# Delta-rule attention and an MLP on one core: odd heads loaded with batch halves swapped, the first chunk's inverse in half units

## The chip, the cores and the metric

The kernel runs on one core of one Trainium2 chip. The metric is device time in microseconds for one execution; the time before is the median of three runs.

## The reference, cut to what matters

Two stages follow each other. The first is a delta rule over 768 steps, for 4 batches and 8 heads of width 48; the second is an MLP over the 3072 tokens that result.

```python
k_n = k / (np.linalg.norm(k, axis=-1, keepdims=True) + 1e-06)
state = np.zeros((B, H, D, D))                         # B, H, S, D = 4, 8, 768, 48
for t in range(S):
    y[:, :, t] = np.einsum('bhd,bhde->bhe', q[:, :, t], state)
    v_old = np.einsum('bhde,bhd->bhe', state, k_n[:, :, t])
    state = state + beta[:, :, t, None, None] * np.einsum('bhd,bhe->bhde', k_n[:, :, t], v[:, :, t] - v_old)
x = y.transpose(0, 2, 1, 3).reshape(B * S, H * D)      # 3072 x 384
out = gelu_tanh(x @ w_in) @ w_out                      # d_ff = 2048
```

## The kernel before

The 768 steps are cut into 12 chunks of 64. A chunk holds 4 batches x 8 heads x 64 steps; two batches are stacked on the 128 partitions (index `a`, 64 rows each), and the other batch index `x` makes two **units** per chunk, so there are 24 units `u` of 8 heads. Heads are numbered by `g` (pair, 0 to 3) and `p` (even or odd within the pair). Work is bf16, sums are float32 in PSUM.

For each unit, `prep(u)` does this. `kn`, `kb`, `qb` make normalised k, k times -beta, and q in token layout (tile `tok`); `T` and `kT` (units 0 to 5, on TensorE with a copy) or `turn` (later units, a transposing DMA on SP) bring them to `kT`. `G2` and `G` (L542, L534) are the products of keys with keys and of keys with queries; `ln` and `wp` are their masked copies. Then comes the inverse of the chunk's triangular matrix, by five Newton steps: `A` multiplies, `rt` (L603, DVE) subtracts from two times the identity, `B` multiplies again, `bde`, `xi` and `bdc` copy the result back to be the next left factor. In units 2 and up these are full-array matmuls on block-diagonal tiles `bd` (L596); `X1` makes the first one. In units 0 and 1 (`TILED`) they run as 64x64 matmuls on two corners of the array (`At`, `Bt`, L567; start `X1t`, L558).

For each chunk, `chain(c)` does this. `K` (L642) multiplies keys by the state, `R` subtracts v, `Um` or `U` (L665) applies the inverse, `S` (L675) makes the state's update, `Q` (L642) multiplies queries by the state and `O` (L689) adds the part inside the chunk. `On` copies to `xo`, then `turnx` (a transposing DMA, L702) or `X` (six transposes on TensorE, L710, for chunks 0, 1 and 11) make `xT`.

In a 64x64 matmul the row half is set by the partitions of the operands and the column half by the partitions of the output. `K`, `Q` and `S` use all four combinations. `O` reads rows `hf(a)` and writes rows `hf(a)`, so it uses the two diagonal corners.

For each chunk the MLP runs as 16 `up` steps (L731, three matmuls of 256 columns each), four `gelu` on ACT, and two times four `down` steps (L743, four matmuls of 384 columns), with `Z` copies and `out` DMAs. The weights W1 and W2 come in two halves each, on GpSimd's DMA queue: `w1.-2.9` is the half that `up.N.5` and `up.N.75` need, `w1.-3` the half for `up.N` and `up.N.25`. In a label such as `up.5.25/0` the first number is 2c+3 for chunk c; for `K`, `Um`, `S` it is 2c+0.5, for `Q` and `O` 2c+0.6 and 2c+0.7, for `X` and `turnx` 2c+0.8.

q, k and v are loaded by SP (the first chunk's k also by ACT): one DMA for each of `a` = 0, 1, with all 16 heads of both units, in pieces of 192 bytes. Each has a ring of three chunks. `norms` takes squares, sums, root (`pow`: on ACT for the first three chunks, on GpSimd later) and reciprocal. The first root needs another activation table than the copy `tmpl` ahead of it.

The order on each engine is written out by hand, as the lists `ORDER["pe"]`, `["act"]`, `["dve"]`, `["pool"]`, `["sp"]`; `BANKS` gives the PSUM banks in order. Each engine works its list strictly in order and waits at each entry for what it reads. `fill` entries (71 of them, L428) are matmuls on zeros that only fill idle time on TensorE before W1 is there.

The lines around O, before:

```python
def at(name, P, r, b, x, g):
    o = 512 * b + 4 * D * x + D * g
    return P(ps(name))[r, o:o + D]
...
def omat(e, P):
    for x, g in each:
        for p in range(2):
            for a in range(2):
                ins = e.matmul(at("O", P, hf(a), p, x, g), wp[ss[x]][hf(a), 4 * p + g, C:2 * C], ub[hf(a), x, p, g, :],
                               start=first and x == 0 and g == 0, stop=True, skip_group_check=True)
```

Of the kernel before, what the change touches and what calls it, by code (L numbers as in the profile page):

```python
# [30 lines left out]
        A32.4/0 up.5.5/0 up.5/3 up.5.5/1 up.5.5/2 A16.5/0 up.5.5/3 B.4/4 A.6/0 B.5/3 down.6.5/0 B.6/0 down.6.54/0 A32.5/0 G2.8/0
        G2.7/0 A.6/1 B.5/4 down.6.58/0 G.8/0 down.6.62/0 Um.4.5/0 B.6/1 Q.4.6/0 G.7/0 O.4.7/0 G2.9/0 A.6/2 A.8/0 down.6/0 A.7/0 B.6/2
        G.9/0 B.8/0 down.6.04/0 B.7/0 down.6.08/0 A.9/0 A16.6/0 A.8/1 down.6.12/0 A.7/1 B.9/0 B.8/1 up.7.25/0 B.7/1 up.7.25/1 B.6/3
        up.7/0 up.7.25/2 up.7/1 up.7.25/3 A32.6/0 up.7/2 A.7/2 up.7/3 A.9/1 A.8/2 S.4.5/0 up.7.5/0 B.9/1 up.7.5/1 B.7/2 up.7.75/0
        up.7.5/2 up.7.75/1 up.7.5/3 up.7.75/2 A16.7/0 up.7.75/3 A.9/2 K.6.5/0 B.7/3 B.6/4 B.8/2 B.9/2 down.8/0 A32.7/0 down.8.04/0
        B.7/4 down.8.08/0 A16.8/0 down.8.12/0 Um.6.5/0 B.8/3 Q.6.6/0 G2.10/0 O.6.7/0 G.10/0 A16.9/0 down.8.5/0 G2.11/0 S.6.5/0 G.11/0
        down.8.54/0 down.8.58/0 B.9/3 A32.8/0 A.10/0 down.8.62/0 K.8.5/0 B.10/0 B.8/4 up.9.75/0 up.9.25/0 up.9.75/1 up.9.25/1
        up.9.75/2 A.10/1 up.9.75/3 A32.9/0 up.9.25/2 A.11/0 B.10/1 up.9.25/3 up.9.5/0 B.9/4 up.9.5/1 G2.13/0 up.9.5/2 up.9.5/3 G.13/0
        Um.8.5/0 Q.8.6/0 B.11/0 A.10/2 G.12/0 G2.12/0 O.8.7/0 A.13/0 B.10/2 up.9/0 up.9/1 B.13/0 A.11/1 up.9/2 A16.10/0 up.9/3 A.12/0
        B.11/1 A.13/1 S.8.5/0 B.10/3 B.13/1 B.12/0 A.11/2 down.10/0 A.12/1 down.10.04/0 B.11/2 down.10.08/0 up.11.75/0 B.12/1  # L40
        up.11.75/1 A.13/2 up.11.75/2 up.11/0 up.11.75/3 B.13/2 up.11/1 A.12/2 A32.10/0 up.11/2 up.11.25/0 up.11/3 up.11.25/1 A16.11/0
        up.11.25/2 B.12/2 up.11.25/3 up.11.5/0 B.11/3 down.10.12/0 up.11.5/1 K.10.5/0 B.10/4 up.11.5/2 A32.11/0 A16.13/0 up.11.5/3
        down.10.5/0 B.11/4 A16.12/0 down.10.54/0 B.13/3 B.12/3 down.10.58/0 Um.10.5/0 down.10.62/0 G2.14/0 Q.10.6/0 S.10.5/0 O.10.7/0
        G.14/0 A32.13/0 down.12/0 A32.12/0 down.12.5/0 B.13/4 down.12.04/0 A.14/0 down.12.08/0 G2.15/0 G.15/0 K.12.5/0 down.12.54/0
        B.12/4 down.12.12/0 B.14/0 down.12.58/0 Um.12.5/0 down.12.62/0 up.13.75/0 Q.12.6/0 G2.17/0 O.12.7/0 G.17/0 up.13.75/1 A.15/0
        up.13.75/2 up.13/0 A.14/1 up.13/1 up.13.75/3 up.13/2 up.13.5/0 up.13/3 up.13.5/1 B.15/0 up.13.5/2 B.14/1 up.13.5/3 up.13.25/0
        G.16/0 G2.16/0 up.13.25/1 up.15.5/0 up.13.25/2 S.12.5/0 up.13.25/3 up.15.5/1 A.15/1 up.15.5/2 A.16/0 A.14/2 up.15.5/3 A.17/0
        B.15/1 down.14/0 B.16/0 B.14/2 down.14.04/0 B.17/0 A.16/1 down.14.08/0 A.15/2 down.14.12/0 A.17/1 B.16/1 up.15/0 B.15/2
        up.15/1 B.17/1 up.15/2 A16.14/0 A16.15/0 up.15/3 up.15.25/0 A.16/2 up.15.25/1 B.14/3 up.15.25/2 A.17/2 up.15.25/3 B.15/3
        B.16/2 K.14.5/0 A32.14/0 up.15.75/0 B.17/2 up.15.75/1 G2.18/0 up.15.75/2 A16.16/0 up.15.75/3 A32.15/0 A16.17/0 B.14/4 B.16/3  # L50
        B.15/4 down.16/0 G.18/0 G2.19/0 down.14.5/0 Um.14.5/0 down.14.54/0 B.17/3 down.16.04/0 S.14.5/0 G.19/0 Q.14.6/0 down.14.58/0
        down.16.08/0 A.19/0 A.18/0 O.14.7/0 K.16.5/0 down.14.62/0 A32.17/0 B.18/0 B.19/0 down.16.12/0 down.16.5/0 B.17/4 A.18/1
        A32.16/0 down.16.54/0 A.19/1 down.16.58/0 B.18/1 G2.20/0 G.20/0 B.16/4 down.16.62/0 up.17.5/0 B.19/1 up.17.5/1 Um.16.5/0
        up.17.5/2 A.20/0 up.17.5/3 up.17.75/0 G2.21/0 up.17.75/1 B.20/0 up.17.75/2 up.17.25/0 up.17.75/3 up.17.25/1 A.19/2 up.17.25/2
        A.20/1 up.17.25/3 Q.16.6/0 G.21/0 O.16.7/0 up.17/0 B.19/2 up.17/1 A.18/2 up.17/2 B.20/1 up.17/3 A16.19/0 B.18/2 S.16.5/0
        A.21/0 B.19/3 down.18/0 A.20/2 down.18.04/0 B.21/0 A16.18/0 B.20/2 down.18.08/0 A.21/1 down.18.12/0 B.18/3 A16.20/0 A32.19/0
        B.21/1 up.19/0 up.19.5/0 up.19/1 B.20/3 up.19/2 B.19/4 up.19/3 up.19.5/1 A.21/2 up.19.5/2 K.18.5/0 up.19.5/3 B.21/2 A32.18/0
        down.18.5/0 up.19.25/0 B.18/4 up.19.25/1 A16.21/0 G2.22/0 up.19.25/2 Um.18.5/0 up.19.25/3 down.18.54/0 B.21/3 Q.18.6/0 G.22/0
        G2.23/0 O.18.7/0 A32.20/0 down.18.58/0 up.19.75/0 down.18.62/0 up.19.75/1 A.22/0 up.19.75/2 down.20/0 up.19.75/3 B.22/0 G.23/0
        S.18.5/0 down.20.04/0 B.20/4 down.20.08/0 A.23/0 A32.21/0 A.22/1 down.20.12/0 B.23/0 up.21.5/0 B.22/1 up.21.5/1 up.21.75/0  # L60
        B.21/4 up.21.5/2 up.21.75/1 A.23/1 up.21.5/3 K.20.5/0 up.21.75/2 B.23/1 up.21.75/3 up.21.25/0 A.22/2 up.21/0 up.21.25/1
        up.21/1 B.22/2 A.23/2 up.21.25/2 up.21/2 up.21.25/3 B.23/2 down.20.5/0 Um.20.5/0 up.21/3 down.20.54/0 A16.22/0 A16.23/0
        down.20.58/0 B.22/3 down.22.5/0 B.23/3 down.22.54/0 Q.20.6/0 S.20.5/0 O.20.7/0 down.20.62/0 A32.23/0 A32.22/0 K.22.5/0
        down.22/0 B.23/4 down.22.04/0 B.22/4 down.22.58/0 down.22.08/0 Um.22.5/0 down.22.12/0 Q.22.6/0 down.22.62/0 O.22.7/0 up.23.5/0
        up.23/0 up.23.5/1 up.23/1 up.23.25/0 up.23.5/2 up.23/2 up.23.5/3 up.23/3 up.23.25/1 X.22.8/0 up.23.25/2 up.23.75/0 up.23.25/3
        up.23.75/1 down.24/0 up.25.75/0 up.25.25/0 up.25.75/1 up.25.25/1 up.25.75/2 up.23.75/2 up.25.75/3 up.25.25/2 up.23.75/3
# [243 lines left out]
def bass_deltanet__then__act_gelu_tanh_kernel(  # L310
# [13 lines left out]
    NU = 2 * NC  # L324
    DIRECT = lambda u: (2, 3, 4, 5) if u < 8 else (2, 4)
    GROUPS = [[c] for c in range(NC)]
    TURN, TURNX, TILED = 6, 2, 2

    F = Flow()
    A = F.add  # L330

    with nc.allow_non_contiguous_dma("strided loads"), nc.allow_low_precision("bf16 pipeline"):
# [39 lines left out]
        def hf(a, n=C):  # L372
            return slice(64 * a, 64 * a + n)
# [437 lines left out]
```

## Time and profile before

| | before |
|---|---|
| median of 3 runs | 265.88 us (265.6 to 266.23) |
| profiled execution | 266.2 us, span 264.4 us |
| PE, DVE, ACT, POOL busy | 253.8, 202.0, 174.8, 144.5 us |
| granted TensorE clock | 1.0 |
| `fill` on PE | 71, 21.8 us |
| DMAs issued by SP | 148 |
| HBM read, written | 20.64 MB, 4.72 MB |

The span runs from the first to the last instruction; the rest of the profiled execution's time lies around it. PE is TensorE; a matmul is counted busy from its start to its modelled end, and neighbours overlap. A line of a group gives the source line, engine, operation, what it writes and reads, its shape, the count, then busy time and the mean of one in ns, then idle time ahead of it and who ended that. In the slices each digit is a fortieth of the span in tenths. "SPq" and "POOLq" are the queues of SP and GpSimd.

### The profile page before, as it was taken

The page shows a single profiled execution, that of the slowest core. Times are in us where ns is not written, and L with a number is a line of the kernel's source. Part 1 is how long each engine was busy: PE and PEld are TensorE (multiplying, and loading weights), DVE is VectorE, ACT ScalarE, POOL GpSimd, SP SyncE. Part 2 cuts the span into 40 slices and gives each one's busy share as a digit, 9 for nine tenths or more (in the row PEclk, how much of TensorE's full clock was granted, in tenths as well). Part 3 has the DMA queues.
Part 4 walks back from the last instruction along what each step waited for, and adds up shares of the span by engine and source line. Part 5 has one row for each costly group of instructions (what it writes and reads, how often), then busy time and mean ns, then how long its engine had stood idle before and what let it go on. Part 6 is the DMA issues. An engine that isn't in the chain of part 4 may idle for free.

```text
span 264.4 us, 12466 instructions
## 1 busy us (share of the span) xinstructions
PE 253.8 (96%) x5629; PEld 191.6 (72%) x5629; DVE 202.0 (76%) x317; ACT 174.8 (66%) x264; POOL 144.5 (55%) x220
## 2 busy tenths in 40 slices
PE   7899998999899999999999999999999999999994
PEld 2557566877677876877886888877888878778762
DVE  8899796978899999899779888889886876551000
ACT  3758676777886894498663468935788657556431
POOL 8633698849899889875855674480635222110000
PEclk9999999999999999999999999999999999999999
DMA  5996999999999999948997589238149064044023
GB/s 105 175 154 124 146 204 193 177 134 151 158 164 155 141 162 137 188 88 165 169 173 100 125 165 147 48 81 144 25 63 180 5 133 82 2 35 101 6 47 72
DMA packets 117908, 31.86 MB, mean 120 GB/s; under 512 B 111968, under 2 KB 117088, under 8 KB 117856
## 3 DMA queue, kind: packets, MB, share of 16 engines
q1 hardware_dynamic: 113968, 27.63, 69.7%
q0 software_dynamic: 2880, 3.15, 7.6%
q8 instruction: 44, 0.72, 1.2%
q10 hardware_dynamic: 1008, 0.30, 0.5%
q14 instruction: 8, 0.07, 0.1%
HBM read 20.64 MB, written 4.72 MB: 96 GB/s over the span
## 4 chain that ended last, share of the span: by engine, by line
PE 78%; DVE 7%; DMA 5%; ACT 2%; SPq 2%; issue 2%; POOL 2%; POOLq 0%; ACTq 0%
PE ps L743 23%; PE ps L731 21%; PE ps L596 18%; DMA W<-in_moe_w_in_dram 4%; PE ps L428 3%; PE ps L567 3%; PE ps L642 2%; DMA kraw<-in_k_dram 2%; DVE ln L546 2%; PE ps L689 2%; SPq L523 2%; PE ps L534 2%; PE ps L665 1%; DVE rt L603 1%; PE ps L542 1%
## 5 line engine op out<-in xcount | busy, mean ns | idle before, releaser
L731 PE MATMUL ps<-xT,W 128*128 128x256 bf16 x576 | 82.4, 273 | 0.8 <-DMA W<-in_moe_w_in_dram 0.7
L376 ACT ACTIVATE bd<-ps 64x512 bf16<-64x512 f32 x111 | 64.5, 589 | 18.0 <-PE ps L596 16.0
L743 PE MATMUL ps<-W,gT 128*128 128x384 bf16 x384 | 76.3, 326 | 0.0
L736 ACT ACTIVATE gT<-ps 128x1024 bf16<-128x1024 f32 x48 | 48.4, 1021 | 27.0 <-PE ps L731 26.6
L731 PEld LDWEIGHTS ps<-xT,W 128*128 128x128 bf16 x576 | 48.7, 98 | 9.5 <-DMA W<-in_moe_w_in_dram 1.0
L603 DVE TENSOR_TENSOR rt<-ps,two 128x512 bf16<-128x512 f32 x66 | 44.2, 687 | 10.6 <-PE ps L596 9.9
L590 POOL COPY bd<-xi 64x256 f32<-64x256 f32 x64 | 25.1, 394 | 42.4 <-ACT xi L376 30.2
L743 PEld LDWEIGHTS ps<-W,gT 128*128 128x128 bf16 x384 | 32.3, 97 | 15.0 <-ACT gT L736 0.2
L586 POOL TENSOR_SCALAR_AFFINE_SELECT bd<-ln 64x512 bf16<-64x512 bf16 x44 | 28.9, 658 | 22.5 <-DVE ln L546 18.4
L376 DVE CAST bd<-ps 64x512 bf16<-64x512 f32 x45 | 30.8, 686 | 5.1 <-PE ps L596 3.9
L552 DVE CAST_PREDICATED wp<-mup,ps 128x1024 bf16<-128x1024 uint16 (+1 forms) x26 | 29.3, 1133 | 2.3 <-PE ps L534 2.3
L489 POOL TENSOR_TENSOR nrm<-nrm,half 128x16 f32<-128x16 f32 x9 | 26.3, 2929 | 2.1 <-DVE nrm L486 1.9
L376 ACT ACTIVATE xi<-ps 128x512 bf16<-128x512 f32 x31 | 18.3, 594 | 12.1 <-PE ps L596 6.9
L596 PE MATMUL ps<-rt,bd 128*128 128x64 bf16 x528 | 25.5, 194 | 0.3 <-DVE rt L603 0.2
L596 PE MATMUL ps<-wp,bd 128*128 128x64 bf16 (+1 forms) x528 | 24.7, 188 | 1.0 <-issue 0.5
L596 PEld LDWEIGHTS ps<-wp,bd 128*128 128x128 bf16 x528 | 21.3, 97 | 5.5 <-issue 1.1
L596 PEld LDWEIGHTS ps<-rt,bd 128*128 128x128 bf16 x528 | 21.1, 98 | 5.0 <-DVE rt L603 2.4
L603 DVE TENSOR_TENSOR rl<-ps,two 128x384 bf16<-128x384 f32 (+1 forms) x44 | 20.8, 485 | 4.8 <-PE ps L596 4.4
L428 PE MATMUL ps<-wz 128*128 128x512 bf16 x71 | 21.8, 413 | 1.3 <-DVE wz L382 1.2
L510 POOL TENSOR_TENSOR tok<-kraw,nrm 128x384 bf16<-128x384 f32 x21 | 17.6, 841 | 8.4 <-DVE nrm L493 8.1
L546 DVE CAST_PREDICATED ln<-mlo,ps 128x512 bf16<-128x512 uint16 x24 | 16.5, 687 | 4.9 <-PE ps L542 4.6
L512 POOL TENSOR_TENSOR tok<-tok,bsb 128x384 bf16<-128x384 bf16 x21 | 17.5, 836 | 2.7 <-DVE tok L510 1.9
(98 smaller groups left out, 334.5 us busy)
## 6 DMA issues: line engine op xcount, KB each, us to landing
qraw<-in_q_dram SPq DMA_DIRECT2D x24, 192.0 KB, 5.1
vraw<-in_v_dram SPq DMA_DIRECT2D x24, 192.0 KB, 4.9
out_dram<-ob SPq DMA_DIRECT2D x47, 96.0 KB, 2.6
kraw<-in_k_dram SPq DMA_DIRECT2D x22, 192.0 KB, 5.3
W<-in_moe_w_in_dram POOLq DMA_DIRECT2D x2, 768.0 KB, 9.2
W<-in_moe_w_out_dram POOLq DMA_DIRECT2D x2, 768.0 KB, 10.8
kraw<-in_k_dram SPq DMA_DIRECT2D x3, 96.0 KB, 4.0
kT<-tok SPq DMA_TRANSPOSE x18, 5.0
```

The source lines that it names most:

```text
L376: return e.activation(out, in_, ACT.Copy) if e is nc.scalar else e.tensor_copy(out, in_)
L428: return e.matmul(P(f"fill{i}")[:, :], wz[:, 0:128], wz[:, 0:512])
L489: e.tensor_tensor(nr[:, 1, hx], nr[:, 0, hx], half[:, hx], ALU.pow),
L546: A("dve", z + "ln", lambda e, P: e.copy_predicated(ln[m][:, :, :].rearrange("p (x g) t -> p x g t", x=2), mlo[:, :].bitcast(U16).unsqueez ...
L552: A("dve", z + ("wp" if nh == 2 else "wph"), lambda e, P, cs=cs, nh=nh: e.copy_predicated(wp[s][:, :, cs], mup[:, cs].bitcast(U16).unsquee ...
L586: A("pool", z + "X1", lambda e, P, src=src, dst=dst: e.affine_select(out=dst, in_=src, compare_op=ALU.not_equal, fill=1.0, base=0, pattern ...
L590: A("pool", z + "bdc", lambda e, P, src=src, dst=dst: e.tensor_copy(dst.bitcast(F32), src.bitcast(F32)), reads=[w("xi")], writes=[n(f"bd{a ...
L596: ins = e.matmul(P(name)[:, C * h + lo:C * h + C], bd[s][:, h, :], rhs[:, h, lo:C])
L603: A("dve", z + f"rt{lo or str()}", lambda e, P, i=i, lo=lo, r_=r_: e.tensor_tensor(r_[:, :, lo:C], P(ps(f"A{i}")).rearrange("p (h t) -> p ...
L731: ins = e.matmul(P(ph)[:, w * f:w * f + w].rearrange("p (x t) -> p x t", x=2), W1[:, j, 128 * (i + f):128 * (i + f) + 128], x_[:, :, j, :] ...
L736: A("act", z + "gelu", lambda e, P, i=i, ph=ph: e.activation(g_[:, i:i + nf, 0:w], P(ph).rearrange("p (f t) -> p f t", f=nf), ACT.Gelu_app ...
L743: ins = e.matmul(P(po)[:, 0:DM], g_[:, f, 128 * b:128 * b + 128], W2[:, f, :], start=(f == 0), stop=(f == FC - 1))
```

## The change

Five things are done together.

1. **Loads.** For odd heads (`p` = 1) the two stacked batches change places: rows `hf(a)` hold batch `a ^ p`. So each load becomes four DMAs, one for each `p` and `a`, of half the size; beta's copy follows the same pattern in four pieces. With the batches swapped, `O` and `Q` write odd heads to rows `hf(a ^ p)`, so that `O` uses all four corners and its output stands in the right order. `K`, `S` and the inverse work as before on swapped rows.
2. **First chunk in halves.** In units 0 and 1 the transposes, the products, the masked copies, all five Newton steps and their copies are cut into two halves of four heads (`Ath`, `Bth`, `rth`, `xih`, `lnh`, `wphh`, `X1h`), each with a PSUM bank of its own; U, O, X and their copies of chunk 0 are cut by unit `x` (`Uh`, `Oh`, `Xh`, `Unh`, `Onh`, `xTh`).
3. **Table.** `tmpl` now reads `one`, which `tabS` writes, so that the root's table is loaded first.
4. **`TURNX`** goes from 2 to 1: chunk 1's output is turned by DMA on SP, not on TensorE.
5. **Orders and banks** are new for all engines. `fill` goes from 71 to 59 entries, SP's DMAs from 148 to 220. Copies are placed anew between ACT and DVE (`bde` on DVE 45 to 39, on ACT 111 to 117).

The core of the diff:

```diff
-    TURN, TURNX, TILED = 6, 2, 2
+    TURN, TURNX, TILED, SPLIT = 6, 1, 2, 2
...
-                    for a in range(2):
+                    for p, a in quad:
+                        dst = raw[n][s][hf(a), :, :].rearrange("t (x g p) d -> t p x g d", x=2, p=2)[:, p, xs]
...
-                          lambda e, P, n=n, a=a, xs=xs, view=view: e.dma_start(raw[n][s][hf(a), xs, :], view[a, c, :, xs, :]), ...
+                          lambda e, P, a=a, p=p, xs=xs, dst=dst, view=view: e.dma_start(dst, view[a ^ p, c, p, :, xs]),
...
-                A("pe", z + "T", trans, reads=[n("tok0"), n("tok1"), n("tok2"), "ident"], alloc=(ps("T"), 2), mode="m", pos=u, mm=12)
+                for ys, tn in (((0, 1), "T"), ((2,), "Tq")) if u < SPLIT else (((0, 1, 2), "T"),):
...
+                    for y, _, k_ in halves:
+                        def product(e, P, name, rhs, lo, y=y):
+                            for h in range(4):
+                                for a in range(2):
+                                    ins = e.matmul(P(name)[hf(a), C * h + lo:C * h + C], xi[m][hf(a), 4 * y + h, :], rhs[hf(a), 4 * y + h, lo:C])
...
-                        ins = e.matmul(at(name, P, hf(a), p, x, g), kT[ss[x]][hf(p, D), y, g, hf(a)], so[hf(p, D), a, x, g, :],
+                        ins = e.matmul(at(name, P, hf(a ^ p if y else a), p, x, g), kT[ss[x]][hf(p, D), y, g, hf(a)], so[hf(p, D), a, x, g, :],
...
-            def omat(e, P):
+            def omat(e, P, xs=(0, 1)):
                 for x, g in each:
-                    for p in range(2):
-                        for a in range(2):
-                            ins = e.matmul(at("O", P, hf(a), p, x, g), wp[ss[x]][hf(a), 4 * p + g, C:2 * C], ub[hf(a), x, p, g, :],
-                                           start=first and x == 0 and g == 0, stop=True, skip_group_check=True)
+                    for p, a in quad if x in xs else ():
+                        ins = e.matmul(at("O", P, hf(a ^ p), p, x, g), wp[ss[x]][hf(a), 4 * p + g, C:2 * C], ub[hf(a), x, p, g, :],
+                                       start=first and g == 0, stop=True, skip_group_check=True)
```

The new orders where the prediction speaks of them:

```diff
 pool
-  ... X1t.0/0 X1t.1/0 kn.3/0 kb.3/0 kb.2/0 kn.4/0 w1.-2.9/0 X1.2/1 X1.2/0 qb.5.01/0 X1.3/1 w1.-3/0 kn.5/0 X1.3/0 pow.6/0 w2.-2/0 ...
+  ... X1h.0/0 X1h.0/1 X1h.1/1 bdz.3/0 X1h.1/0 kn.3/0 kn.2/0 qb.3.01/0 kb.2/0 X1.2/0 X1.2/1 w1.-2.9/0 X1.3/1 qb.4.01/0 X1.3/0 sq.6/0 w1.-3/0 w2.-2/0 ...
 pe
-  ... X.0.8/0 B.2/1 A.3/0 fill/64 fill/65 fill/66 up.3.5/0 A.2/2 B.3/0 up.3.5/1 B.2/2 up.3.5/2 fill/67 up.3.5/3 up.3.25/0 A.3/1 S.0.5/0 ...
+  ... S.0.5/0 Xh.0.8/1 G.4/0 B.2/1 fill/53 fill/54 A.3/1 up.3.5/0 up.3.5/1 A.2/2 B.3/1 up.3.5/2 fill/55 up.3/0 B.2/2 up.3/1 A.3/2 up.3.5/3 ...
```

More of the change, by code (lines that the diff above doesn't have):

```diff
@@ new lines @@
+        xih.0/4 xih.1/3 sq.4/0 kT.2/0 pow.4/0 xih.0/5 ladj16.-0.2/0 kT.3/0 xih.0/7 xih.1/7 xih.1/6 xih.0/6 R0.0.5/0 xih.0/9 xih.0/8
+        Unh.0.5/0 R0.0.5/1 bde.2/0 bde.2/1 Onh.0.7/0 Unh.0.5/1 sq.8/0 xTh.0.8/0 Onh.0.7/1 bde.3/1 tabG.3/0 S0.0.5/0 xTh.0.8/1 bde.2/2
+        bde.2/3 bde.3/3 bde.2/4 gelu.3.5/0 gelu.3/0 gelu.3.25/0 bde.2/6 bde.3/4 bde.3/5 gelu.3.75/0 bde.4/0 bde.3/6 bde.4/1 bde.2/9
+        bde.2/8 bde.3/8 bde.4/3 Un.2.5/0 On.2.7/0 sq.12/0 bde.4/5 bde.4/4 sq.10/0 bde.5/1 bde.5/0 sq.14/0 Z.4.5/0 bde.4/6 bde.5/3
@@ L115 @@
-        Sn.20.5/0 rt32.23/0 rt32.22/0 R.22.5/0 bde.22/4 Z.22/0 xT.22.8/0 Z.24.5/0
+        wz.-200/0 bdz.4/0 pad.-9/0 bdz.2/0 bdz.7/0 one.-40/0 sqh.0/0 identf.-29/0 sumh.0/0 eps.0/0 ladj16.0.8/0 inv.0/0 kn.0/0
+        betaN.-28/2 betaN.-28/3 betaN.-28/1 betaN.-28/0 ladj16.2.8/0 kb.0/0 sumh.1/0 eps.1/0 inv.1/0 kn.1/0 kb.1/0 lnh.0/1 lnh.0/0
+        wphh.0/0 sum.-140/0 wphh.0/1 lnh.1/1 rth.0/0 lnh.1/0 rth.0/1 eps.-140/0 wphh.1/1 wphh.1/0 inv.-140/0 qT.0/0 rth.0/3 rth.1/1
+        rth.0/2 rth.1/0 kb.3/0 ladj16.1.8/0 rth.1/3 rth.0/4 rth.1/2 wph.1/0 rth.0/5 xih.1/2 wph.0/0 ladj32.2.8/0 sum.4/0 rth.1/4
@@ L116 @@
+        bde.21/3 bde.18/4 rt16.21/0 Un.18.5/0 Z.18.5/0 ln.22/0 wp.22/0 ln.23/0 rt32.21/0 rt.22/0 bde.21/4 wp.23/0 Sn.18.5/0 rt.23/0
+        rt32.20/0 rt.22/1 bde.23/0 bde.20/4 rt.23/1 R.20.5/0 rt.22/2 rt.23/2 rt16.22/0 rt16.23/0 Z.20.5/0 xi.22/1 Sn.20.5/0 rt32.22/0
+        rt32.23/0 R.22.5/0 bde.23/5 On.22.7/0 xT.22.8/0
     """,
     "pool": """
[L118 to L119 removed]
@@ L410, in preset @@
                 A("pool", "0tmplz", lambda e, P: e.memset(tmpl[:, C:2 * C], 0.0), writes=["tmplz"], pos=-11)
-                A("act", "0tmpl", lambda e, P: e.activation(tmpl[:, 0:C], two[:, :], ACT.Copy, scale=-0.5), reads=["two"],
+                A("act", "0tmpl", lambda e, P: e.activation(tmpl[:, 0:C], two[:, :], ACT.Copy, scale=-0.5), reads=["two", "one"],
                   writes=["tmpl"], pos=-11)
@@ L618, in chain @@
             n = lambda y: [f"{y}{s}" for s in ss]
[L619 to L620 removed]
+            inv = n("bd0") + n("bd1")
             ps = lambda y: f"{y}.{c}"
@@ L636, in at @@
                 o = 512 * b + 4 * D * x + D * g
-                return P(ps(name))[r, o:o + D]
+                return P(ps(name) if name != "O" or not first else ps(f"O{x}"))[r, o:o + D]
             def ks(e, P, y, name):
```

429 lines of the change are left out of this document (230 added, 199 removed), and 16 rows, old and new, of the table BANKS.

## The prediction, made before any run of the changed kernel

> **What bounds the kernel now.** I read the busy table and the slices first, then the chain of waits, then the groups by form, then the timelines of TensorE (PE) and of the queues.
>
> ```profile
> PE 253.8 (96%) x5629; PEld 191.6 (72%) x5629; DVE 202.0 (76%) x317; ACT 174.8 (66%) x264; POOL 144.5 (55%) x220
> ...
> DMA  5996999999999999948997589238149064044023
> ```
>
> PE is busy for 96% of 264.4 us. Busy is not yet pace, so I looked at spacing in the timeline: three `up` matmuls start 0.33 us before the next instruction and four `down` ones 0.65 us, early and late alike. After the prologue PE works near its own pace. The second line shows DMA full (nines) from 6.6 to about 105 us.
>
> ```profile
> 33.33 9.55 DMA W<-in_moe_w_in_dram
> 42.93 0.50 PE ps L731 x3
> 45.55 0.76 PE ps L731 x6
> ```
>
> This is the chain that ended last. Up to 42.93 us it waits for one half of W1 (`w1.-3`), issued by GpSimd at 33.33; from there it is nearly all PE. So the end is set by when W1 lands and by how much PE work is left then.
>
> ```profile
> L642 PE MATMUL ps<-st,kT 48*64 48x48 bf16 x704 | 9.7, 189 | 0.0
> ...
> L689 PE MATMUL ps<-us,wp 64*64 64x48 bf16 x384 | 8.3, 187 | 0.3
> ...
> L675 PE MATMUL ps<-us,tok 64*64 64x48 bf16 x352 | 4.8, 188 | 0.2 <-ACT us L376 0.2
> ```
>
> Groups by form: K and Q (L642), O (L689), S (L675) are all 32 matmuls of 48 columns. O uses two corners of the array, the others four. One O takes 8.3/12 = 0.69 us, one S 4.8/11 = 0.44, one K or Q 9.7/22 = 0.44.
>
> **O on four corners.** Chunks 1 to 11 have one O each in the PE-bound part: 11 x (0.69 - 0.44) = 2.8 us less. The first chunk's O lies in the prologue and counts there. Against it could count that the new O lets both row halves write each bank, where S keeps them apart; if the halves then wait for each other, O stays at 0.69. A row speaks to that: the first chunk's U (L665, 64*64) has both row halves writing one bank on two corners, and its 32 take 0.7 us; the full-array Um takes 6.2/11 = 0.56 us for 16, of which some 0.16 is the tail that S loses when another tiled step follows (0.28 to the next start, against its 0.44), so 25 ns each. One after the other, 32 would take 0.96: the halves overlap while sharing a bank. The Trainium skill, TensorEngine Tiling (Array Packing), Gotcha 1, says that different row tiles cannot access the same PSUM bank simultaneously; by that O would stay at 0.69, and U's row does not agree with it. I take 0.44 and keep 0.69 as a rival.
>
> **Transposes of chunk 1.** X.2.8 leaves PE (six matmuls, 61.48 to 61.81 in the timeline): 0.33 us less. It becomes `turnx.2.8` on SP, whose others issue in 1.2 and land in 3.1 us. Between O.2.7 and the next `up` the new order has six `down` (3.9 us), six A or B steps of 0.23, and G and S: over 6 us, against 0.8 (copy) + 3.1 plus any queueing. Hidden if SP comes to it in time; if not, PE waits for the difference.
>
> **The head of the kernel.** `tabS` first removes the 1.28 us table load that stands between sum and root at 5.93. But k of chunk 0 now comes in four quarters per half, two behind each other on each queue: issue at 1.6 plus 4.0 to land is 5.6, against 4.2 to start with before (work on it began at 4.77). 5.6 + 0.49 (square) + 0.55 + 0.21 + 0.18 + 0.18 + 0.56 (kn) and steps between gives 8.3 instead of 8.8. The four betaN of half size (two took 0.73) and kb end near 10.0 instead of 10.52. The halved transposes and the copy of 1024 elements on ACT (1.04) bring `lnh.0` to 12.2 to 12.9, say 12.6, against 13.35.
>
> **The first inverse in halves.** DVE is what it runs on. From `ln.0` to the end of `ln.2` it took 27.70 - 13.35 = 14.3 us. After: 23 operations of 256 elements at 0.34 (row of 128x256: 0.42 busy, 0.08 of it overlapped) = 7.8; four of 192 at 0.28 = 1.1; two `wph` 1.2; two sums 1.7; small norms 0.5; qT and kb.3 0.75; three `ladj` 0.45; a `tri` 0.4; `ln.2` 0.6: 14.5 us, so it ends at 27.1, with a few waits 27.1 to 28. Splitting gives each chain shorter steps, but as many elements and more starts on the busy engine. `X1.2` (two of 0.66) then lets `w1.-2.9` go at 28.5 to 29.5 on POOL; it went at 28.72. `w1.-3` comes after X1.3, qb.4 and now sq.6 (1.46): ln.3 ends near 29.7, so 33 to 34 instead of 33.33. The first half landed at 37.5 and the second followed 5.4 later, so an issue up to about 35 costs nothing. W1 thus lands at 42.9 to 43.7: I take 0.4 us later.
>
> Ahead of it much is gained and not cashed: rt.2, wp.3 and two copies (2.4) after 29.7, then U, Unh, Oh, Onh, Xh, xTh in halves (2.7 against 5.3 from U to `up` before) put `up.3.5/0` at 34.8 instead of 39.38, but its half of W1 lands at 37.5, and the new order asks for the other half (`up.3/0`) three `up` later, near 39. PE then waits 4 us. What it did before the wait differs from the old list by S, A.3/1, B.3/1 (+0.83) less B.2/2 and an `up` (-0.56): 0.27 us less left. The twelve fills removed covered idle time and cost nothing.
>
> **Loads cut in two.** 72 more DMAs on SP (148 to 220), as many bytes and packets. With nothing queued an issue takes 0.6 us whether it carries 192 or 96 KB, so SP has up to 43 us more to issue. Adding up its timeline gives 19 of the first 20 us, 18 of the next 40, 85 of the 100 us from 60 to 160, and 37 after. Many early issues are long (1.0 to 2.3 us) because the full DMA queues push back, and that part is set by bytes. I take nothing for it, at most 5 us.
>
> **Other orders.** DVE hands some 5 us of copies after the prologue to ACT and SP (bde 45 to 39 at 0.69, two xT, one Un), which can take a little from waits on DVE near 113 to 120 us. I take nothing for it; a saving of up to 1 us lies in the range.
>
> **Sum.** -2.8 - 0.33 - 0.27 + 0.4 = -3.0 us. The profiled execution took 266.2 (span 264.4 and 1.8 around it), 0.3 above the median 265.88, so 263.2 on its scale and 262.9 on the median's; I say 263.1. A measurement of this kernel can tell about 0.2% (0.53 us) from no change.
>
> **Rivals.**
> - W1 comes sooner. If the halved chains reach `ln.2` 2 to 3 us earlier (each half operation at 0.25 rather than 0.34 saves 2), W1 is issued and lands as much earlier: 260.6. Against it: the DVE rows show no such rate from PSUM, and W1's two halves need 14 us of shared DMA. 10%.
> - The idle gap slows PE's clock. The first 15 fills take 5.23 us, the 11 from 8.00 take 2.55, so 15 at that later pace take 3.5: a cold start costs about 1.8 us. At the end the granted clock in the windows is 1.00 up to 264.0 and 0.98 in the last 0.4, some 3.5 us after PE's last matmul. A wait of 4 us at `up.3/0` could bring one more slow start: 265.0. No wait in this trace is that long, so nothing shows it mid-kernel. The Trainium skill, TensorE: Matmul & The Clock Gate, HAM oscillation, states as a rule that PE gaps should stay below about 3.4 us, and by it this would happen. 14%.
> - O gains nothing: both row halves wait for each other at the shared bank, and 2.8 stays: 265.9, no change. 6%.
> - Slower: SP becomes the bound from 60 to 160 us. About half of the extra loads fall there; at 0.6 us, 36 of them add 21 to the 85, which makes 106 of 100. SP is in order, so `turn` (landing 5.0) and `turnx` come up to 6 us late by the end of that stretch, and PE waits at G2 and `up`: 263.1 + 5 = 268. It decides where halved loads keep 0.6 us and the pushed-back part (some 27 us: the 85 less 51 loads and stores at 0.6, 14 `turn` at 1.4 and 6 `turnx` at 1.2) shrinks by less than 6. For it: the queue's order is fixed, and DVE, ACT and POOL also wait in order for what it loads. Against: the push-back should shrink by more than that. 18%.
>
> **Chances.** The forecast has 52%. Faster by over 0.2%: 0.52 + 0.10 + half of the clock case (0.07) = 0.69. Within: 0.07 of the clock case and 0.04 of O = 0.11. Slower: SP 0.18 and 0.02 of O with a late W1 = 0.20. The range holds the forecast with the early-W1 end, the clock case, O and the start of the SP case: 260.2 to 266.9.
>
> **What would show it.** Right: O (32 matmuls) at 0.44 us in the groups by form; `lnh` of unit 0 near 12.6; `w1.-2.9` issued near 29 and the `up` after it waiting for W1 until 43 with some 4 us idle; PE busy total down by the fills and O; the chain still PE after 43. Wrong: O at 0.69; W1 landing before 41 or after 45; granted clock below 1.00 near 44; PE idle before L542 or L731 with DMA named between 60 and 160 us, or chain shares of SPq and DMA above the present 2% and 5%.

## The result, and the profile after

The changed kernel takes 276.8 us against 266.1 beside it: ratio 1.040 (95% interval 1.033 to 1.047). It is slower by some 11 us; 263.1 was forecast, and the range ended at 266.9. The profiled execution took 277.71 us, its span 276.0. (Runs in which the chip was disturbed are left out of all ratios; medians hold them.)

The busy table, the granted clock, the DMA share and the shares of the chain, from the page of the changed kernel; the second fence has the chain's line of the kernel before:

```profile
PE 254.1 (92%) x5643; PEld 190.5 (69%) x5643; DVE 196.6 (71%) x327; ACT 178.6 (65%) x279; POOL 145.8 (53%) x226
...
PEclk9999986999999979999999999999999999999999
DMA  6877899989998988897776947646608622124004
...
PE 66%; DMA 13%; POOL 8%; SPq 6%; issue 2%; ACT 2%; DVE 1%; POOLq 0%; ACTq 0%
```

```profile
PE 78%; DVE 7%; DMA 5%; ACT 2%; SPq 2%; issue 2%; POOL 2%; POOLq 0%; ACTq 0%
```

PE is busy for as long as before in a span 11.6 us longer. Its share of the chain fell from 78% to 66%; DMA rose from 5 to 13, SP's queue from 2 to 6, POOL from 2 to 8. Many of the nines of the DMA row have become sevens and eights: the transfers fill their engines less, though more of them are issued.

The chain of waits, the pieces in order of time (start, us, what):

```profile
29.45 8.46 DMA kraw<-in_k_dram
37.99 1.41 POOL sq L497
39.40 8.76 DMA W<-in_moe_w_in_dram
...
59.36 1.42 SPq L470
61.49 4.70 DMA kraw<-in_k_dram
66.37 5.04 DMA xT<-xo
...
91.41 5.08 DMA xT<-xo
```

Where before had one wait for W1 there are now loads. k of chunk 3, the last of its four DMAs issued at 29.45, lands 8.5 us later; `sq.6` on POOL needs it and stands in front of `w1.-3`, which goes at 39.40, not 33.33. DVE, in order, stands at `sum.6` until 39.49 (the first line below, with 4.66 us idle ahead of it), with `rt.2/1` behind it (the second), and PE behind that:

```profile
39.49 1.81 DVE L498 TENSOR_REDUCE nrm<-sq 128x16 f32<-128x768 f32 x2 [4.66 <-POOL sq L497]
41.22 0.68 DVE L635 TENSOR_TENSOR rt<-ps,two 128x512 bf16<-128x512 f32 x1
```

Then SP's own issues (SPq) are a piece of the chain, and `turnx.2.8` and `turnx.4.8` (66.37, 91.41) come late. What PE waited for between 34 and 100 us (us in total, times, longest), and the windows around 40 us and behind the second late `turnx` (third number from the end: granted clock):

```profile
PE ps L782 <- DMA xT<-xo: 4.7, 2, 3.2
PE ps L758 <- DVE rt L635: 2.7, 1, 2.7
PE ps L716 <- issue: 2.2, 1, 2.2
```

```profile
38.00:40.00 2.00, 0.30 (x13) 0.20 (x13) 0.51 (x1) 1.36 (x3) 2.00 (x2) 0.89 0.55 102
40.00:42.00 2.00, 0.00 (x0) 0.00 (x0) 2.00 (x4) 0.23 (x1) 1.98 (x3) 0.50 0.76 106
42.00:44.00 2.00, 1.66 (x28) 1.20 (x29) 1.35 (x2) 0.49 (x1) 2.00 (x1) 0.50 1.03 182
44.00:46.00 2.00, 2.00 (x15) 1.23 (x14) 1.03 (x2) 1.18 (x2) 1.83 (x4) 0.50 1.07 185
```

```profile
97.00:100.00 3.00, 3.00 (x34) 2.43 (x32) 0.00 (x0) 1.66 (x3) 1.38 (x3) 0.60 0.90 159
```

The granted clock is half from 40 to 46 us; PE is idle for the first 2 of these and works at half its clock for the rest. Behind the 3.2 us that PE waited for `turnx.4.8` it falls again, to 0.60 between 97 and 100 us. By `down.4.12`, at 62.05 us before, the changed kernel is 6.5 us behind, by `down.8`, at 95.88 before, 11.4; after that it stays there (11.5 at the end).

The groups by form: K and Q, O, S.

```profile
L673 PE MATMUL ps<-st,kT 48*64 48x48 bf16 x704 | 9.7, 188 | 0.0
L729 PE MATMUL ps<-us,wp 64*64 64x48 bf16 x384 | 5.6, 188 | 0.4 <-issue 0.3
L716 PE MATMUL ps<-us,tok 64*64 64x48 bf16 x352 | 5.2, 188 | 2.3 <-issue 2.2
```

O did nearly what was said of it: 5.6/12 = 0.47 us in place of 0.69, where 0.44 was forecast.

### The profile page after: what moved, and what is told of

Its sections match the earlier page's. It is cut to its first block, busy times and chain, and to the rows that moved or that the text cites. A ratio compares the mean times of both kernels' runs of the same rounds, so it can differ in the third digit from the quotient of the medians.

```text
span 276.0 us, 12596 instructions
## 1 busy us (share of the span) xinstructions
PE 254.1 (92%) x5643; PEld 190.5 (69%) x5643; DVE 196.6 (71%) x327; ACT 178.6 (65%) x279; POOL 145.8 (53%) x226
## 3 DMA queue, kind: packets, MB, share of 16 engines
q0 software_dynamic: 2880, 3.15, 7.5%
## 4 chain that ended last, share of the span: by engine, by line
PE 66%; DMA 13%; POOL 8%; SPq 6%; issue 2%; ACT 2%; DVE 1%; POOLq 0%; ACTq 0%
PE ps L782 22%; PE ps L794 17%; PE ps L628 15%; SPq L470 6%; DMA kraw<-in_k_dram 5%; DMA xT<-xo 4%; DMA W<-in_moe_w_in_dram 3%; PE ps L437 2%; PE ps L673 2%; POOL nrm L501 2%; POOL tok L522 2%; POOL bd L618 2%; PE ps L552 1%; DMA braw<-in_beta_dram 1%; PE ps L560 1%
## 5 line engine op out<-in xcount | busy, mean ns | idle before, releaser
L782 PE MATMUL ps<-xT,W 128*128 128x256 bf16 x576 | 83.3, 277 | 5.0 <-DMA xT<-xo 4.7
L385 ACT ACTIVATE bd<-ps 64x512 bf16<-64x512 f32 x117 | 67.6, 590 | 25.0 <-PE ps L628 23.0
L782 PEld LDWEIGHTS ps<-xT,W 128*128 128x128 bf16 x576 | 49.6, 99 | 12.8 <-issue 3.3
L385 DVE CAST bd<-ps 64x512 bf16<-64x512 f32 x39 | 26.7, 684 | 6.1 <-PE ps L628 5.6
L582 DVE CAST_PREDICATED wp<-mup,ps 128x1024 bf16<-128x1024 uint16 x22 | 26.6, 1212 | 2.3 <-PE ps L552 2.3
L385 ACT ACTIVATE xi<-ps 128x512 bf16<-128x512 f32 (+1 forms) x41 | 20.4, 517 | 10.5 <-PE ps L628 5.5
L524 POOL TENSOR_TENSOR tok<-tok,bsb 128x384 bf16<-128x384 bf16 x19 | 16.0, 842 | 9.3 <-PE ps L716 4.6
L437 PE MATMUL ps<-wz 128*128 128x512 bf16 x59 | 18.9, 430 | 1.3 <-DVE wz L391 1.2
L567 DVE CAST_PREDICATED ln<-mlo,ps 128x512 bf16<-128x512 uint16 (+1 forms) x26 | 16.7, 645 | 3.1 <-PE ps L560 2.8
L522 POOL TENSOR_TENSOR tok<-kraw,nrm 128x384 bf16<-128x384 f32 x20 | 16.5, 837 | 2.4 <-DVE nrm L505 2.2
## 6 DMA issues: line engine op xcount, KB each, us to landing
W<-in_moe_w_out_dram POOLq DMA_DIRECT2D x2, 768.0 KB, 10.4
```

Source lines behind the costliest of these rows:

```text
L385: return e.activation(out, in_, ACT.Copy) if e is nc.scalar else e.tensor_copy(out, in_)
L437: return e.matmul(P(f"fill{i}")[:, :], wz[:, 0:128], wz[:, 0:512])
L522: A("dve" if u < 2 else POOL, z + "kn", lambda e, P: e.tensor_tensor(kn, kr, nr[:, 3, hx].unsqueeze(2).to_broadcast(full), ALU.mult), read ...
L582: A("dve", z + "wp", lambda e, P: e.copy_predicated(wp[s][:, :, :], mup[:, :].bitcast(U16).unsqueeze(1).to_broadcast([128, H, 2 * C]), P(p ...
L782: ins = e.matmul(P(ph)[:, w * f:w * f + w].rearrange("p (x t) -> p x t", x=2), W1[:, j, 128 * (i + f):128 * (i + f) + 128], x_[:, :, j, :] ...
```

## The experiments

Theory A: the doubled number of load issues on SP costs the time, by making loads late; B and its kin (the rivals): the halved inverse, the orders, or single wrong places in them.

| run | what | us | ratio to before (95%) |
|---|---|---|---|
| e_plain | changed kernel, two loads a tensor | 265.5 | 0.994 (0.988-1.000) |
| b_O2 | before, O on four corners, its own loads | 265.2 | 0.991 (0.986-0.995) |
| b_O4 | the same, four loads a tensor | 279.5 | 1.049 (1.043-1.055) |
| e_15_1 | four loads, cut 15 heads and 1 | 285.5 | 1.074 (1.067-1.081) |
| e_head | changed kernel, two loads, O as before | 268.7 | 1.004 (1.000-1.008) |
| p_c0_4 | e_plain, four loads for chunks 0-4 | 271.2 | 1.015 (1.010-1.021) |
| p_c5_7 | for chunks 5-7 | 267.8 | 0.999 (0.995-1.004) |
| p_c8_11 | for chunks 8-11 | 268.0 | 1.001 (0.996-1.006) |
| e_k3early | changed kernel, k of chunk 3 sooner | 276.4 | 1.035 (1.028-1.041) |
| e_korder | k of chunks 3 and 4 sooner | 276.9 | 1.040 (1.033-1.047) |
| e_w1late | W1 behind `sq.6` | 278.0 | 1.043 (1.036-1.050) |
| e_turnx | two `turnx` sooner | 277.6 | 1.036 (1.030-1.043) |
| e_fix | e_korder with `turnx` sooner | 280.5 | 1.052 (1.044-1.059) |
| e_actout | 20 output DMAs on ACT | 281.7 | 1.053 (1.047-1.059) |
| e_out | changed kernel, output DMAs merged | 310.9 | none taken |
| b_out | before, output DMAs merged | 290.8 | 1.092 (1.084-1.101) |
| b_late6 | merged, corner O for chunks 6-11 | 294.6 | 1.107 (1.100-1.113) |
| b_late8n | before, corner O for chunks 8-11 | 269.4 | 1.006 (1.002-1.010) |

The us column has medians of runs taken at different times; compare by the ratios. e_plain, b_O2, e_15_1 and the three p_ kernels leave out the swapped loads that the corner O needs (the p_ kernels for some chunks): they time the same work, but their output is not the reference's.

**The number of loads.** e_plain goes back to the loads of before, with everything else of the change kept:

```diff
-                    for p, a in quad:
+                    for a in range(2):
-   e.dma_start(dst, view[a ^ p, c, p, :, xs])
+   e.dma_start(raw[n][s][hf(a), xs, :], view[a, c, :, xs, :])
```

> The changed kernel with the loads of before: two DMAs of 192 KB for each tensor of a chunk (rows of both heads in place, not swapped) in place of four of 96 KB, each pair at the last two places that its four had in SP's list (k of chunk 0: the first two). The rows of odd heads then belong to the other batch half, so its output is not the reference's; every other instruction is the same. Theory A (the doubled count of issues on SP, 0.64 us each, is the cause of both late steps): k of chunk 3 is there before X1.3 ends, sq.6 does not wait, the first half of W1 is issued at 33 to 35 and lands at 42 to 44; turnx.2.8 and turnx.4.8 are issued within 1.5 us of O's copy; time 262 to 265 us, at or below the kernel before (266). Rival B (the count is harmless, and the first inverse in half units, or the new orders, cost the time by themselves): 272 us or more, the wait of sq.6 or of rt.2/1 still there.

Theory A held, at the upper end of its 262 to 265 us: 4.6% (1.040 less 0.994) or 12 us hang on the loads' count. The second half of W1 was issued at 33.75 and landed at 43.10, as said. b_O2 puts O alone into before; b_O4 adds the loads (`for p, a in quad`, as in the change), beta's copy in four pieces, and changes no order:

```diff
-   ins = e.matmul(at("O", P, hf(a), p, x, g), wp...
+   ins = e.matmul(at("O", P, hf(a ^ p), p, x, g), wp...
```

> The kernel before with one part of the change alone: the eleven later O (and Q that fills the same tile) write row half a^p, so that O's 32 matmuls use all four corners. Its loads, orders and instruction counts are those of before; the rows of odd heads are not swapped, so its output is not the reference's. Theory: O goes from 0.69 to 0.44-0.47 us, 11 x 0.23 = 2.5 us less, 263.2 to 263.8. Rival (O is faster but what follows it waits for the same copy, load or turn, or matmuls of two row halves on one bank hold each other up): 265 to 266.2, no change.

> The kernel before with O on four corners and the loads and betaN of the change (swapped rows, four DMAs of 96 KB a tensor, each pair standing where one DMA of 192 KB stood); the first inverse, the root's table and all other orders as before. Its output is the reference's. Theory A (the count of issues is what costs, whichever first inverse and order stand around it): the loads before W1 come in at 0.50 to 0.56 MB in 4 us in place of 0.60 to 0.67, chunk 0's k lands later, and what b_O2 gained (-0.9%) is lost and more: 268 to 274. Rival (before's orders have the slack on SP, the change's new orders have not): 263 to 265.5.

O alone is worth 0.9% (2.4 us); with the doubled loads, before's own orders lose 5.8% (1.049 less 0.991), no less than the new orders do. That is the direction of theory A, but more than the 268 to 274 us that it gave for b_O4. e_15_1 keeps count, bytes and places but not the swapped rows:

```diff
-   for p, a in quad: dst = ...[:, p, xs]
+   for p, a in quad: xs = slice(h0, h1 - 1) if p == 0 else slice(h1 - 1, h1)
```

> The changed kernel with its own places in SP's list and four DMAs a tensor, but cut otherwise: rows are not swapped, and each half's load is cut into fifteen heads (180 KB) and one head (12 KB) in place of eight and eight (for the first chunk's k seven and one). As many issues, as many bytes; the rows of odd heads belong to the other batch half, so its output is not the reference's. Theory A4 (SP's time for an issue, 0.64 us whatever its size, is what costs: 74 more issues, of which some 55 before 150 us, where SP has no break): 274 to 280, like the changed kernel. Rival E (the swapped rows, an odd stride of heads or the landing of 96 KB pieces cost): 264 to 268, like the run with two DMAs a tensor.

The swapped rows are thus not the cause. That it is slower by another 3.4% (some 9 us) was not expected. Some 3 us of it arise at the head: the last k of chunk 3 is issued at 32.16 us and lands at 41.05, 3.1 later than in the changed kernel, and the first `up` starts 3.15 later (48.24 against 45.09). The rest is not explained. SP's issues of k in the changed kernel and in e_plain (min/median/max ns), then the rate in their windows from 4 to 28 us, the last number, GB/s:

```profile
L470 SPq DMA_DIRECT2D kraw<-in_k_dram x47: 595/635/1416, 0.8 to 126.4; - x47
```

```profile
4.00:28.00 24.00, 22.47 (x488) 13.87 (x487) 21.69 (x63) 15.61 (x33) 12.63 (x21) 1.00 0.81 140
```

```profile
L466 SPq DMA_DIRECT2D kraw<-in_k_dram x24: 595/1006/4122, 0.8 to 115.7; - x24
```

```profile
4.00:28.00 24.00, 21.23 (x482) 13.76 (x487) 21.89 (x63) 14.34 (x32) 12.53 (x20) 1.00 1.23 161
```

96 KB in 0.64 us is 154 GB/s at best from SP. The 192 KB issues can be as short (0.595 us); most are longer, and the DMA share beside them is 1.23 against 0.81 (the number before the rate), so we read the difference as full DMA queues that push back: there the transfers wait, not SP. In the changed kernel SP issues for 18.1 of the first 20 us and 10.4 of the next 11, before for 18.4 and 7.3. So the halved loads make SP the limit from the first microsecond, and until 28 us data arrive 13% slower than in e_plain (140 against 161).

**The first inverse and the orders alone.** e_head also undoes the corner O (`hf(a ^ p)` back to `hf(a)`).

> The changed kernel without swapped rows and corner O (two loads a tensor in e_plain's places, O, Q and beta as before): the first inverse in half units, the root's table first and the new orders alone. Output is the reference's. Theory A6 (the 2.6 us gained by the first inverse are given back before 60 us, since W1 and the chunk behind set the first ups, and PE's idle time there brings the half clock; the rest is O): 267 to 268.5 (ratio 1.002 to 1.008), O at 0.69 us, the first up at 40 to 43 and the clock under 0.9 between 38 and 44 us. Rival J (the first inverse is worth its 2.6 us, and O's gain is what is lost in e_plain): 263.5 to 265.

Theory A6 held in the time, in its reasons only in part. The clock stayed at 1.00. The inverse of chunk 1 starts 2.9 us sooner (`A.2/0` at 29.61 against 32.55), and at the first `down`, near 53 us, the kernel is no longer ahead of before but 0.7 us behind; the first `up` started at 40.78, yet PE did not wait for W1. The chain from 36 to 42 us runs through chunk 3's root on POOL and, in DVE's new order, through `inv.6` and `wp.4` to the `rt` that PE needs:

```profile
36.39 2.94 POOL nrm L497
39.33 0.48 POOL tok L382
...
40.19 0.25 DVE nrm L501
40.45 1.08 DVE wp L578
41.53 0.60 DVE rt L631
```

e_plain less e_head is 1.1% (2.8 us; the two intervals together allow 0.4 to 1.8%), which fits O once more (e_head, then e_plain):

```profile
L725 PE MATMUL ps<-us,wp 64*64 64x48 bf16 x384 | 8.4, 187 | 0.3 <-PE ps L669 0.2
```

```profile
L725 PE MATMUL ps<-us,wp 64*64 64x48 bf16 x384 | 5.5, 188 | 0.3 <-PE ps L669 0.2
```

**Where the count costs.** Four loads for some chunks, two for the others (`for p, a in quad if c in (0, 1, 2, 3, 4) else ...`):

> The kernel of e_plain (the changed kernel with two loads a tensor, 265.5 us; rows of those chunks not swapped, so the output is not the reference's), but with the change's four loads a tensor for chunks 0 to 4 alone (34 issues more, all but some ten before 45 us). Theory A5 (half of the loss arises before 60 us, where loads that are not in by 31 us wait behind W1): 269 to 272, the first up at 43 to 46 and the rest in step with e_plain. Rival G (the dense stretch behind 45 us makes all of it): under 267.

> The same with four loads a tensor for chunks 5, 6 and 7 alone (18 issues more, 35 to 130 us; output not the reference's for the same reason). Theory A5: the other half of the loss arises between 60 and 110 us, where SP has no break: 268 to 271, with turnx.2.8 or turnx.4.8 late at PE. Rival G2 (SP catches up in its waits for buffers): under 266.5.

> The same with four loads a tensor for chunks 8 to 11 alone (24 issues more, from 83 us on; output not the reference's). Theory A5: behind 110 us the changed kernel loses nothing more to the kernel before, so these cost little: 265 to 267.5. Rival (each added issue costs 0.15 us wherever it stands): 269.

(The first has 32 more in fact, 3 of them on ACT.) Against e_plain they lose 2.2, 0.6 and 0.7%, each within 0.7 to 0.8, so that only the first is clear of noise. Chunks 0 to 4 make near half of the 4.6%, and theory A5 holds there; 5 to 7 alone cost less than it said. The sum is 3.5%; the rest would arise only where all stand together, but lies within what the intervals allow. POOL's wait in p_c0_4, 28 to 50 us, and its window at half clock:

```profile
POOL sq L504 <- DMA kraw<-in_k_dram: 6.4, 1, 6.4
```

```profile
40.00:44.00 4.00, 1.42 (x26) 0.99 (x27) 3.62 (x5) 0.49 (x1) 3.98 (x3) 0.50 0.90 141
```

**Can the order mend it?** Five kernels change the order alone: four move late loads or turns forward on SP, e_w1late moves the first issue of W1 back on POOL (shortened):

```diff
 e_k3early  sp: loadk.2/0 + loadk.2/2 loadk.2/3 (from 8 and 13 places behind)
 e_korder   sp: load.-38/0 + load.-38/2, loadk.2/*, loadk.4/*, then q of chunk 2
 e_w1late   pool: - w1.-2.9/0 X1.3/1 qb.4.01/0 X1.3/0 sq.6/0   + X1.3/1 qb.4.01/0 X1.3/0 sq.6/0 w1.-2.9/0
 e_turnx    sp: turnx.2.8/0 before turn.6/0, turnx.4.8/0 behind loadk.12/1
 e_fix      sp: as e_korder; turnx.2.8/0 before turn.6/0, turnx.4.8/0 behind turn.9/0
```

> The changed kernel with one thing moved: the last two DMAs of k of chunk 3 (loadk.2/2 and /3) are issued on SP right behind loadk.2/0, some 7 us sooner, the other loads 1.3 us later. Theory A1 (that k, landing at 37.9 beside W1, holds sq.6, and with it w1.-3 and, through sum.6, rt.2/1 and the first up): k lands near 30, sq.6 runs at 32.5 to 34, W1's first half is issued at 33.5 to 34.5 and lands at 42.5 to 44, the first up starts at 37 to 40 in place of 45.1; about 5 to 7 us of 277 are gone, to 270 to 272, with the late turnx still in it. Rival B1 (the first up waits for something else, such as S.0.5's gap or the tiles of Xh): the first up at 43 or later and less than 2 us gained. Rival C1 (an earlier end of this stage meets the late turnx harder, SP being the bound after 45 us): the gain of the head is given back by 66 us, total within 2 us of 277.

> The changed kernel; on SP the rest of v of chunk 0 and all of k of chunks 3 and 4 go ahead of the last three DMAs of q of chunk 2, of q of chunk 3 and of v of chunk 1; nothing else moves. The run with k of chunk 3 alone moved showed that the wait went to the next tensor (k of chunk 4, 4.6 us of ACT, landing 39.6). Theory A3 (half-size loads are issue-bound on SP until 31 us, and what has not landed when W1 starts to flow waits until its half is over): now nothing that is needed before 39 us is behind W1; sq.6 at 32 to 33, sq of chunk 4 on ACT at 35, rt.2/1 at 35 to 38, the first up at 37 to 41, and 4 to 7 us less than 276.8: 270 to 273. Rival B3 (a further tensor takes the wait's place, q of chunk 2 or v of chunk 1): first up at 43 or later, 275 to 278.

> The changed kernel with the issue of W1's second half (w1.-2.9, the one that goes first) moved on POOL from before X1.3 to behind sq.6; the loads stay as they are. Theory A3 (W1's packets hold up the loads that are queued on the same DMA engines): with no W1 in flight k of chunk 3, issued at 29.4, lands within 3.5 to 4.5 us (32.9 to 34) in place of 8.5; sq.6 waits under 2 us; W1's two halves are issued at 34 to 36 and land at 43 to 53, the first up at 43 to 46; total 273 to 278. Rival D (the load is slow for itself, being the thirty-ninth of SP's queue): it still lands 7 us or more behind its issue.

> The changed kernel with only turnx.2.8 (ahead of turn.6) and turnx.4.8 (ahead of three loads) moved forward on SP. Theory A2 (PE's waits of 1.5 us at 71.5 and 3.2 us at 96.5, with the clock at 0.60 behind the second, are SP's queue): turnx.2.8 issued 2.5 to 3.5 us sooner, turnx.4.8 2 to 3 us sooner, both waits of PE under 0.5 us, 3 to 5 us of 277 gone: 272 to 274. Rival B2 (turn.6, or a later load that is now behind, becomes late instead): less than 1 us gained, PE or POOL waiting at another load.

> The kernel of e_korder with turnx.2.8 ahead of turn.6 and turnx.4.8 right behind turn.9 on SP. Theory A3 with A2: the head as there, and PE's two waits for xT of chunks 1 and 2 (1.5 and 3.2 us, with the lower clock behind them) are gone: 266 to 269. Rival (SP, 0.64 us an issue and without a break from 45 to 160 us, makes other transfers late in their place): within 1.5 us of e_korder.

None gains clear of noise. What each was meant for came true at its place (but for the first `up` in e_k3early, still at 45.26, and for `turnx.4.8` in e_turnx, for which PE still waited 2.3 us), and the next item of the queue was late in its place. In order: DVE in e_k3early, 30 to 50 us, where ACT's square now waits for k of chunk 4; POOL in e_korder, 40 to 60 us, at q of chunk 3; POOL in e_fix, 60 to 110 us, at k of chunk 8, since SP stood from 83.4 to 86.7 at the `turnx` that now came first; and PE behind that.

```profile
DVE nrm L503 <- ACT sq L501: 4.2, 1, 4.2
```

```profile
POOL tok L390 <- DMA qraw<-in_q_dram: 4.7, 1, 4.7
```

```profile
POOL sq L502 <- DMA kraw<-in_k_dram: 7.3, 1, 7.3
```

```profile
PE ps L633 <- POOL bd L627: 5.5, 1, 5.5
```

e_w1late shows how W1 enters. Without it in flight the same load lands 2.9 us after its issue (issued at 29.71; `sq.6` starts at 32.67), and POOL waits:

```profile
POOL sq L502 <- DMA kraw<-in_k_dram: 0.6, 1, 0.6
```

So 5.6 of the 8.5 us were W1's doing. But W1 then lands later, PE waits 3.4 us for it, and nothing is won.

**Relief for SP.** e_actout gives 20 output issues to ACT; e_out and b_out make one DMA of an output tile's two; b_late6 adds corner O for chunks 6 to 11 to that, b_late8n for 8 to 11 to before as it is.

```diff
 e_actout  act: Z.4.5/0 + out.4.5/0 out.4.5/1 (and nine more tiles)
 e_out     - two e.dma_start(out[r0:r0 + C, :], o_[hf(a), :])
           + e.dma_start(out as [2, 64, 384], o_[:, :])
 b_late*   swp = c >= SWAP; four loads, hf(a ^ p) in O and Q, so[.., a ^ p ..] in K, Q and S where swp
```

> The changed kernel with 20 of the 48 output DMAs (those of the ten output tiles before 170 us that ACT copies out of PSUM) issued by ACT right behind its copy, in place of SP; transfers, sizes and all else as they are. Theory A4 (time on SP is short): SP gains 20 x 0.6 = 12 us and the waits for ACT's copies that stood in its queue; 3 to 6 us come back: 271 to 274. Rival H (not SP's time but the landing of the loads is short): 276 to 279, or later by ACT's 12 us more.

> The changed kernel with SP relieved elsewhere: the two DMAs of each output tile (96 KB each) are one of 192 KB, at the later one's place; 23 issues fewer, some 10 of them before 165 us. Theory A4: SP gains 0.6 us for each of these, 2 to 6 us of 277 come back: 271 to 275. Rival F (SP waits for buffers and not for its own issues): 276 to 278.

> The control for it: the kernel before with the same merged output. Theory A4: before has SP issues to spare, and the merged output leaves it where it is: 265 to 267 (ratio 0.995 to 1.005). If SP bounds before too, 261 to 264.

> A version meant to keep the gain without its price: the kernel before with merged output, and swapped rows and O on four corners for chunks 6 to 11 alone (their tensors in four loads, 36 issues more, nearly all behind 60 us; the states stay in batch order by exchanging the two banks that odd heads' S writes and K and Q read). Output is the reference's. Theory A4: 6 x 0.23 = 1.4 us gained, 36 issues more against 23 fewer on SP, of which some cost: 264 to 267. Rival (any added issue before 150 us costs in full, 0.15 to 0.2 us each as 74 did 11 to 14): 267 to 271.

> The kernel before with swapped rows and O on four corners in chunks 8 to 11 alone (24 issues more, from some 80 us on; outputs in two DMAs as before; the states stay in batch order). Output is the reference's. Theory A5: 4 x 0.23 = 0.9 us gained, and the added issues cost as much or more where SP has no break (p_c8_11: 2 us): ratio 0.997 to 1.006, no version that beats before for certain. Rival (before's own order has room for them): ratio 0.994 to 0.997.

e_actout is 3.5 us ahead of the changed kernel at `down.8`, near 104 us, near the gain that theory A4 asked for; then it loses 7, and its total misses the 271 to 274 us of A4 by far. From 110 us to the end PE waits for ACT, 6.8 us over several rows (the changed kernel: 0.3); the two longest:

```profile
PE ps L632 <- ACT bd L389: 2.9, 2, 1.8
PE ps L786 <- ACT bd L389: 1.7, 1, 1.7
```

The merged output relieves nothing: e_out's profiled run took 305.8 us, and even before gets 9% slower (b_out). One merged DMA has two as its outer dimension; in b_out's trace its 128 rows of 1.5 KB take 4.2 to 5.1 us where they stand alone, while the 64 rows of one of before's DMAs take as little as 0.6. So e_out, b_out and b_late6 say nothing on SP. b_late8n does: 24 issues more (and beta's copy in six pieces for two) cost more than four O of 0.23 us gain. No version was found that beats both kernels and computes the reference; b_O2 has its gain because it leaves out the swapped loads that the corner O needs.

## Why the prediction was wrong

- **O on four corners**: right. 0.47 us (0.44 was said), 2.4 us alone and 2.8 in e_plain, against 2.8. The rival that O gains nothing is out: at the shared bank O did not stay at 0.69. The Trainium skill, TensorEngine Tiling (Array Packing), Gotcha 1, rules out different row tiles on one bank at the same time; O's row after does not agree with it either.
- **Head and first inverse**: right. `lnh.0` started at 12.34 (12.6), `ln.2` ended at 27.77 (27.1 to 28), `w1.-2.9` went at 29.33 (28.5 to 29.5). That the lead could not be cashed was right as well, but not for the reason given: with the loads in time (e_head) chunk 3's norms on POOL and DVE took the place that was given to W1, and the first `up` came at 40.78, not at 34.8.
- **Loads cut in two**: the step that failed. "I take nothing for it, at most 5 us" measured 12 (4.6%, against e_plain). Its working counted SP's free time, "18 of the next 40" us, over a stretch whose loads are needed at its beginning: what matters is the rate up to 31 us, before W1 flows, and there SP had little to spare (19 of the first 20 us taken, and 10.4 of the next 11 after the change). And it took the long issues for time set by bytes that would shrink as the count rose. They did shrink, to 0.64 us, but two of these are 1.28 against 1.01 for one (medians of k's issues, after and e_plain).
- **"An issue up to about 35 costs nothing"**: the time that it rested on failed: `w1.-3` went at 39.4, not at 33 to 34. The step priced `sq.6` at its 1.46 us and never asked when its k would be there. DVE's `sum.6` ahead of `rt.2/1` was the second wait added by the same load, and it was not named.
- **`turnx.2.8`**: the condition, "Hidden if SP comes to it in time", failed. PE waited 1.5 us, and 3.2 at `turnx.4.8`, with the lower clock behind it.
- **Rivals**: that SP becomes the bound was the right mechanism, at 18%, with a price of 5 us and a start at 60 us. It begins with the first load, costs near half its price before 60 us, and over 10 in all. In the stretch that it named, 60 to 160 us, SP issued for 92 of the 100 us, not 106: the pushed-back part did shrink there, as was argued against it. The clock rival came true too, as a consequence of the late loads and not of a wait for W1: 0.50 from 40 to 46 us.
- **Other orders**: no gain, as said; with the first inverse they cost 0.4% (e_head, 0.0 to 0.8).

## What to carry to other kernels

Before splitting transfers, add up the issuing queue over the stretch in which the data must be there, at the measured time of one issue, not over the whole kernel. A queue that works in order and is full moves its lateness from one consumer to the next when the order is changed; here five orders gained nothing, and only fewer issues did. Of every operation that moves ahead of a critical issue, ask when its own input lands.

## What the runs showed of the hardware

- An issue takes 0.64 us (medians of k's in the changed kernel) for 48 KB on ACT and for 96 KB on SP alike. In e_15_1, between 6 and 15 us, it takes 0.60 to 0.67 us, for 12 KB and for 180 KB alike.
- While W1 flows, the loads crawl (8.5 us against 2.9 for the same load, above). In the records of before between 32 and 36 us W1's queue moved 344 packets, nearly all of 2 KB, and SP's queue 341, of 192 bytes: one for one, so a tenth of the bytes. The Trainium skill, DMA: Bandwidth & Descriptors, SWDGE vs HWDGE vs iDMA, states that each DMA engine serves its queues in turn; this window agrees. In the changed kernel the same window has 321 packets against 228, which is less even.
- The time of the merged output fits two engines: in b_out 128 packets of 65 ns each (median) are 8.3 us of work, done in 4.2 to 5.1. The Trainium skill, DMA: Bandwidth & Descriptors, Why a DMA increments its semaphore by 16 and not by 1, states that a transfer runs on the largest number of engines, up to 16, that divides the outermost dimension of both sides, here two; the trace agrees.
- Half clock came without a long gap. In e_plain, between 30 and 60 us, PE never waited over 1.8 us, but was busy for only 2.2 of 4 us, and then had 0.50 (first fence); in e_head, 3.0 of 4 busy, it kept 1.00 (second). That is one execution of each:

```profile
36.00:38.00 2.00, 1.05 (x37) 0.89 (x34) 2.00 (x4) 1.96 (x5) 1.30 (x1) 1.00 0.74 105
38.00:40.00 2.00, 1.16 (x33) 0.79 (x34) 1.52 (x3) 1.73 (x4) 2.00 (x2) 0.80 1.07 191
40.00:42.00 2.00, 1.78 (x23) 1.39 (x21) 1.43 (x3) 1.56 (x3) 1.83 (x3) 0.50 1.18 203
```

```profile
36.00:38.00 2.00, 1.32 (x45) 1.17 (x42) 2.00 (x4) 1.82 (x5) 1.61 (x1) 1.00 0.89 151
38.00:40.00 2.00, 1.70 (x41) 0.96 (x42) 1.22 (x2) 1.97 (x4) 1.91 (x3) 1.00 1.11 204
```

- Open: in the changed kernel, e_plain and e_head `S.0.5` stops after 19 of its 32 matmuls for 2.2, 1.8 and 0.7 us ("issue" above), with nothing in the profile to wait for. A transfer of 16 KB of instructions runs just ahead of it or beside it: it ends at 37.86, 37.20 and 36.64 us, and the matmuls go on 1.2, 1.6 and 1.4 us later. In e_w1late, where it ends at 34.51, before `S.0.5` begins, there is no stop. That it is the cause was not tested.
